# Router logits of an attention and expert kernel: split fp32r products against fp32 products in four column quarters

## The chip, the cores and the metric

The kernel runs on one core of one Trainium2 chip. The time is the device time of one execution in microseconds (us), the median of several executions.

## The reference

Eight batches of eight heads of causal attention over 576 positions of 64 numbers, then a two-level mixture of experts on the 4,608 resulting tokens of 512 numbers. All is fp32.

```python
s_pos = np.maximum(s, 0.0); cum = np.cumsum(s_pos, axis=-1)
bias = -(cum[:, :, :, None] - cum[:, :, None, :])
scores = np.where(causal, -1e9, scale * q @ k.T + np.minimum(bias, 0.0))
attn = softmax(scores)                       # max taken off, 1e-9 in the sum
x = (attn @ v) as tokens                     # [4608, 512]
g_logits = x @ w_group                       # 4 groups: argmax and softmax weight
e_logits = x[of group g] @ w_expert[g]       # 4 experts of the group: the same
h = np.maximum(x[of expert] @ w1[g, e], 0.0) # 512 -> 1024
out[of expert] = (g_w * e_w)[:, None] * (h @ w2[g, e])
```

So each token needs 20 logits (4 of the groups, 4 x 4 of the experts), goes through one of 16 experts, and its row is scaled by the product of two softmax weights.

## The kernel before

**Number forms.** TensorE takes fp32 operands whole, or in the form fp32r, which holds fewer bits. Where the kernel wants the accuracy of fp32 from fp32r it splits an operand into a high part (the cast to fp32r) and a low part (the rest) and adds the products high x high, high x low and low x high.

**Attention.** Two heads make a pair; there are 32 pairs, four to a batch. A loop over steps (`for step in [-4, -3] + list(range(NH + 5))`) interleaves several heads: the row maxima of the head four steps on (line 208), the scores of this head (lines 265 and 267), the exponentials (line 275) and the causal zeroes on GpSimd (line 284), and the product with V of the head before (line 305). The order is written out by hand: `ORDERS` holds a list for even and one for odd steps, in which a token with a digit issues one group of matmuls (A row maxima, B scores, C product with V) and a letter pops one deferred piece of work from a queue of its own. `R` takes one turn of the router. PE, DVE, ACT and Pool follow the order in which they are issued; each engine is a queue in order. `ring` hands out the three score banks in turn and first pops the reader of the bank three before. ScalarE's queue also issues two small DMAs a pair (line 243).

**Tokens.** When a pair is done, `turn`, `recip`, `back` and `finish` (letters Y, Z, W, K) make its tokens transposed, `xT`, 128 channels x 576 positions, on VectorE (line 352). Then `high` casts 512 positions to fp32r on ScalarE (X, line 365), `low` subtracts on GpSimd (L, line 370; VectorE for the last two pairs), `tail` copies the last 64 positions on ScalarE (M, line 375), and `rows_out` turns the pair back to rows on TensorE and stores them (O and o, lines 393 and 399). After the fourth pair of a batch, `route` (Q) queues a router batch.

**The router.** `Router.batch` is a generator; each `R` runs it to the next `yield`. `logits` (lines 720, 721, 724) adds eight fp32r matmuls of 512 columns: for each of the four 128-channel chunks the high tokens against high and low weights side by side (52 columns, the low ones from column 32) and the low tokens against the high weights (20 columns). ScalarE copies rows 32 to 52 out (`lo`, line 780), VectorE adds them to rows 0 to 20 (line 782). The 64 tail positions are four fp32 products (line 785) and a copy (line 786). Then the tails are turned to rows and stored (lines 791 to 798), the logits `lT` are turned to tokens in rows by five transposes against the identity (line 803), and VectorE picks groups and experts, counts, and makes lists of tokens (lines 811 to 947). For the last batch the logits of three chunks are issued one pair early.

**Between the stages.** The first expert slot starts while the last batch is routed. Its matmuls and the router's are put in one order of TensorE with `behind(later, earlier)`: the 41st, 53rd and 73rd product of its first layer stand behind the last logits, their turn and the counts, and the ninth of its second layer behind the first list.

**The slots.** One expert after the other, the fullest first. `x_items` turns the gathered rows on VectorE (line 1111) and splits them (high on ScalarE, line 1115; low on VectorE, line 1116), two channel chunks at a time. `h_items` makes eight 128-row blocks of the hidden layer from `xh` and `xl` and the weights `w.h` and `w.l` (line 1155): four chunks of (xh wh, xl wh), then four of xh wl. ReLU and its split follow (`hh` line 1150, `hl` line 1151). `y_items` makes the output (line 1210), or `y_rows` (line 1177) where the slot's size is a multiple of 128. The next slot's gather, turn and weight split run beside this. `beyond`, five VectorE items (lines 1457 to 1461) that test whether a slot overflows, is issued after the sixth block of slot 3.

Of the kernel before, what the change touches and what calls it, by code (L numbers as in the profile page):

```python
# [20 lines left out]
P = 128  # L21
# [90 lines left out]
def attention(tc, qk, v, s, wr, xs, st):  # L112
# [3 lines left out]
    with ExitStack() as ctx:  # L116
# [207 lines left out]
        def normalise(p, vals, sums):  # L324
# [22 lines left out]
            def finish():  # L347
                for k in "OXLM":
                    need(k, p - 2)
                x = m["x"] = sm.tile([P, S], F32, name=f"xT{p}", tag="xT", bufs=2)  # L350
                xTs[p] = x
                product[0] = nc.vector.tensor_tensor(out=x, in0=vals, in1=m["f"], op=ALU.mult)
                push("X", p, high)
                push("O", p, lambda: rows_out(p))

            def high():
                x = m["x"]
                if c == 0:
                    for k in "LMQ":
                        need(k, p - 1)  # L360
                    rt[0].read(p // 4)
                    xhl[p // 4] = [late.tile([P, 4, 512], F32R, name=f"xT{n}{p}", tag=f"xT{n}", bufs=1) for n in "hl"]
                    xtail[p // 4] = late.tile([P, 4, 64], F32, name=f"xtl{p // 4}", tag="xtail", bufs=2)
                xh, xl = (t[:, c] for t in xhl[p // 4])
                st.xh = nc.scalar.copy(xh, x[:, 0:512])
                st.highs.append(st.xh)
                push("L", p, lambda: low(xh, xl, x))

            def low(xh, xl, x):
                st.lows.append((nc.gpsimd if p < NP - 2 else nc.vector).tensor_tensor(  # L370
                    out=xl, in0=x[:, 0:512], in1=xh.bitcast(F32), op=ALU.subtract))
                push("M", p, lambda: tail(x))

            def tail(x):
                nc.scalar.copy(xtail[p // 4][:, c], x[:, 512:576])
                b = p // 4
                if p == NP - 2:
                    push("Q", p, lambda: rt[0].logits(b, *xhl[b], range(3)))
                if c == 3:
                    push("Q", p, lambda: route(b))  # L380

            push("Y", p, turn)

        def route(b):
            rt[0].queue.append(rt[0].batch(b, xtail.pop(b), *xhl.pop(b)))

        def rows_out(p):

            b, c = p // 4, p % 4
            x = xTs.pop(p)  # L390
# [13 lines left out]
        xTs, xtail, xr, xhl = {}, {}, [None], {}  # L404
# [43 lines left out]
        c0, c1 = (late.tile([P, 4, 512], F32R, name=f"c{n}", tag=f"xT{n}", bufs=1).rearrange("p a c -> p (a c)")  # L448
# [7 lines left out]
        wr_f = ac.tile([P, 4, 20], F32, name="wr_f")  # L456
        wr_sb = ac.tile([P, 4, 52], F32R, name="wr_sb")
        nc.scalar.dma_start(wr_f, wr.rearrange("(c p) n -> p c n", p=P))
# [37 lines left out]
        def constants():  # L496
            ones(3)
            rt.append(Router(tc, ac, late, end, kept, ring, wr_f, wr_sb, xs, st))


        def store_sums():
# [137 lines left out]
class Router:  # L639


    def __init__(self, tc, ac, sm, end, ps_t, ps_s, wr_f, wr_sb, xs, st):
        self.end = end
        self.tc, self.sm, self.ps_t, self.ps_s, self.xs, self.st = tc, sm, ps_t, ps_s, xs, st
        self.wr_f, self.wr_sb = wr_f, wr_sb
# [3 lines left out]
        self.lg = {}  # L649
# [21 lines left out]
        self.lT = ac.tile([20, NB * P], F32, name="lT")  # L671
        nc.gpsimd.memset(self.lT[:, S:], 0.0)
        nc.gpsimd.memset(self.wr_sb.bitcast(F32).rearrange("p c n -> p (c n)"), 0.0)
# [38 lines left out]
    def logits(self, b, xh, xl, chunks):  # L712

        nc = self.tc.nc
        if chunks[0] == 0:
            self.lg[b] = self.ps_s(f"lg{b}")
# [967 lines left out]
```

## Time and profile before

| | us |
|---|---|
| median of 3 runs | 917.94 |
| lowest and highest of them | 917.87, 923.0 |
| the profiled execution | 919.4 |
| its span, first to last instruction | 917.6 |

| engine | busy us | share of the span |
|---|---|---|
| PE (TensorE matmul) | 863.2 | 94% |
| PEld (TensorE weight load) | 777.8 | 85% |
| DVE (VectorE) | 701.0 | 76% |
| ACT (ScalarE) | 628.9 | 69% |
| POOL (GpSimd) | 660.5 | 72% |

Matmuls are pipelined and their ends are modelled, so a PE that is busy all the time is not a PE at its peak: where matmuls follow each other, the distance from start to start is the cost of one, not its length. Time that a DMA issue takes on a queue is not counted as busy. The granted TensorE clock was 0.99 of full speed over the span.

### The profile page before, as it was taken

How to read it: one execution, taken by the hardware profiler on the slowest of the kernel's cores; microseconds unless marked ns; L12 is line 12 of the kernel's file. 1: busy time of each engine (PE TensorE's matmuls, PEld its weight loads, DVE VectorE, ACT ScalarE, POOL GpSimd, SP SyncE). 2: the span in 40 equal slices, each digit the busy share in tenths (PEclk: the TensorE clock that was granted, in tenths of full speed). 3: DMA queues.
4: the chain of work that ended last, by engine and by line, in shares of the span. 5: the costliest groups of instructions: out<-in, count | busy, mean ns of one | idle time of the engine just before them, and what ended most of it. 6: DMA issues, size and time to landing. Idle time of an engine off the chain costs nothing. (4 is left out here: it accounts for less than half of the span.)

```text
span 917.6 us, 17751 instructions
## 1 busy us (share of the span) xinstructions
PE 863.2 (94%) x5649; PEld 777.8 (85%) x5649; DVE 701.0 (76%) x1997; ACT 628.9 (69%) x1374; POOL 660.5 (72%) x762
## 2 busy tenths in 40 slices
PE   4899999999999999999999999999999999999993
PEld 3688787887878788887888999999999999999992
DVE  7776685867868686885676798889888889888830
ACT  3688786887878788876846556665767666676640
POOL 8898686867868687763787565666678878877750
PEclk9999999999999999999999999999999999999997
DMA  7766655563555656423556544554645555665410
GB/s 154 180 168 158 151 142 146 142 163 92 157 151 145 145 144 168 109 85 132 161 215 218 179 163 166 193 187 174 224 175 195 186 208 187 230 229 198 171 44 23
DMA packets 65005, 148.10 MB, mean 161 GB/s; under 512 B 7588, under 2 KB 40996, under 8 KB 54728
## 3 DMA queue, kind: packets, MB, share of 16 engines
q1 hardware_dynamic: 55020, 126.98, 46.3%
q0 software_dynamic: 7488, 18.89, 5.6%
q10 hardware_dynamic: 2396, 1.02, 0.4%
q8 instruction: 47, 0.77, 0.4%
q14 instruction: 54, 0.44, 0.2%
HBM read 108.97 MB, written 19.69 MB: 140 GB/s over the span
## 5 line engine op out<-in xcount | busy, mean ns | idle before, releaser
L1042 POOL TENSOR_TENSOR wl<-raw,wh 128x512 fp32r<-128x512 f32 x182 | 232.1, 1297 | 53.6 <-ACT wh L1039 35.4
L159 POOL TENSOR_TENSOR WB<-r,WA 64x576 fp32r<-64x576 f32 x128 | 180.9, 1413 | 23.4 <-PE pm L208 7.2
L216 DVE CUSTOM_DVE_ANT_0 mx<-pm,mask 128x192 bf16<-128x192 f32 (+4 forms) x320 | 129.1, 419 | 39.2 <-PE pm L208 34.6
L1039 ACT CAST wh<-raw 128x512 fp32r<-128x512 f32 x256 | 153.9, 616 | 1.4 <-issue 0.8
L1155 PE MATMUL ph<-xl,wh 128*128 128x256 f32 (+13 forms) x512 | 145.7, 304 | 5.0 <-DVE xl L1116 4.5
L1155 PE MATMUL ph<-xh,wh 128*128 128x256 f32 (+13 forms) x512 | 144.7, 301 | 1.6 <-ACT xh L1115 1.1
L208 PE MATMUL pm<-WA 66*128 66x288 f32 (+4 forms) x384 | 126.0, 356 | 17.5 <-DMA WA<-ch 9.4
L265 PE MATMUL ps<-WA 68*128 68x320 f32 (+4 forms) x384 | 135.3, 356 | 7.1 <-ACT pu L275 3.7
L305 PE MATMUL po<-pt,VT 128*128 128x256 f32 (+3 forms) x512 | 121.2, 353 | 0.5 <-POOL xTl L370 0.5
L1210 PE MATMUL py<-hl,wh 128*128 128x256 f32 (+13 forms) x448 | 113.3, 302 | 1.3 <-DVE hl L1151 1.3
L1210 PE MATMUL py<-hh,wh 128*128 128x256 f32 (+13 forms) x448 | 112.7, 301 | 0.0
L267 PE MATMUL ps<-WB 128*128 128x320 f32 (+4 forms) x384 | 109.8, 299 | 0.0
L1256 DVE STREAM_TRANSPOSE yr<-yT 32x384 f32<-32x384 f32 (+1 forms) x208 | 104.5, 502 | 4.3
L305 PE MATMUL po<-pu,VT 128*128 128x320 f32 (+1 forms) x384 | 107.3, 388 | 0.0
L1111 DVE STREAM_TRANSPOSE xt<-xg 32x256 f32<-32x256 f32 (+1 forms) x208 | 102.5, 493 | 3.2
L1155 PEld LDWEIGHTS ph<-xl,wh 128*128 128x128 f32 x512 | 96.6, 189 | 8.6 <-DVE xl L1116 6.4
L1155 PEld LDWEIGHTS ph<-xh,wh 128*128 128x128 f32 x512 | 96.7, 189 | 3.8 <-ACT xh L1115 2.7
L305 PEld LDWEIGHTS po<-pt,VT 128*128 128x128 f32 x512 | 87.6, 192 | 12.9 <-issue 0.8
L1150 ACT ACTIVATE hh<-ph 128x256 fp32r<-128x256 f32 (+13 forms) x128 | 53.5, 420 | 61.1 <-PE ph L1155 60.4
L208 PEld LDWEIGHTS pm<-WA 66*128 66x128 f32 (+1 forms) x384 | 68.7, 190 | 30.9 <-DVE mc L216 13.7
L1155 PE MATMUL ph<-xh,wl 128*128 128x256 f32 (+13 forms) x512 | 90.1, 299 | 0.0
L284 POOL TENSOR_SCALAR_AFFINE_SELECT pt<-pt 128x128 f32<-128x128 f32 (+2 forms) x192 | 63.7, 342 | 36.5 <-ACT pt L275 31.9
(256 smaller groups left out, 1913.5 us busy)
## 6 DMA issues: line engine op xcount, KB each, us to landing
raw<-in_w_dram SPq DMA_DIRECT2D x64, 1024.0 KB
WB<-WA SPq DMA_DIRECT2D x64, 288.0 KB
r<-in_qk_dram SPq DMA_DIRECT2D x31, 576.0 KB
VT<-in_v_dram SPq DMA_DIRECT2D x32, 384.0 KB
xs<-xr SPq DMA_DIRECT2D x15, 512.0 KB
xs<-xrt SPq DMA_DIRECT2D x7, 128.0 KB
xg<-xs,ids POOLq DMA_INDIRECT x46
out_dram<-yr,ids POOLq DMA_INDIRECT x43
```

The costliest lines, as they stand in the source:

```text
L159: i = nc.gpsimd.tensor_tensor(out=wb[64 * a:64 * a + 64, a, h], in0=r[:, h, a], in1=w[0:64, a, h, QO:].bitcast(F32), op=ALU.subtract)
L208: nc.tensor.matmul(ps[:rows, :cw], WA[i][0:66, QA, h, QO + q0:QO + q0 + rows], WA[i][0:66, KA, h, QO + c0:QO + c0 + cw], start=True, stop= ...
L216: nc.vector.tensor_tensor_reduce(out=tmp[:rows, :cw], in0=ps[:rows, :cw], in1=mk[:rows], scale=1.0, scalar=-3.0e38 if c0 == 0 else mo, op0 ...
L265: nc.tensor.matmul(ps[:rows, o:o + w], WA[i][0:68, KA, h, QO + k0:QO + k0 + rows], WA[i][0:68, QA, h, QO + q0:QO + q0 + w], start=True, st ...
L267: nc.tensor.matmul(ps[:rows, o:o + w], WB[p % NBB][:, KA, h, k0:k0 + rows], WB[p % NBB][:, QA, h, q0:q0 + w], start=False, stop=True)
L305: i = nc.tensor.matmul(po[0][:, qa - base:qb - base], VT[p % NVT].rearrange("p t a d -> p (t a d)")[:, (3 * t + 1 + h) * 64:][:, 0:P], x[: ...
L1039: self.casts.append(nc.scalar.copy(h[:, j], raw[:, j]))
L1042: self.low = nc.gpsimd.tensor_tensor(out=l[:, j], in0=raw[:, j], in1=h[:, j].bitcast(F32), op=ALU.subtract)
L1111: V.transpose(dst[:, 0:n, :, j], src[:, 0:n, :, i])
L1155: self.products.append(nc.tensor.matmul(pss[f][:, :cap], w[f // 4][:, c, (f % 4) * P:(f % 4 + 1) * P], x[:, c, :cap], start=(c == 0 and w ...
L1210: self.products.append(nc.tensor.matmul(pss[c][:, :cap], w[2 + f // 4][:, f % 4, c * P:(c + 1) * P], x[:, f, :cap], start=(f == 0 and w is ...
L1256: V.transpose(dst[:, 0:n, :, i], src[:, 0:n, :, j])
```

## The change

The tokens are no longer split. One tile `xT` of four pairs holds a batch, and `finish` writes a pair's tokens into it; `high`, `low`, `tail` and `route` are gone, and Q now queues the batch and stands in the even steps, after B0 and ahead of a turn of the router. The logits are fp32 products of chunk c with 32 columns of weights (12 of them zero), written to the partitions 32c to 32c + 32 of a bank; no chunk is added to another on TensorE. Two copies on ScalarE bring the four parts to `lT`, now 128 rows. The turn, five fp32 products against `sum4` in place of the transposes, turns the logits and adds the four parts in one. In `item(0)` of a slot's first layer, and in the first block of `y_rows`, the products with the low tokens (low hidden rows) now come last. `beyond` comes after the second block of slot 3. The counts with which the first slot's matmuls stand behind the router's are 35, 46 and 64, and 4.

```diff
             def finish():
-                for k in "OXLM":
-                    need(k, p - 2)
-                x = m["x"] = sm.tile([P, S], F32, name=f"xT{p}", tag="xT", bufs=2)
-                xTs[p] = x
+                b = p // 4
+                if c == 0:
+                    rt[0].read(b - 1)
+                    need("O", p - 5)
+                    xTs[b] = late.tile([P, 4, S], F32, name=f"xT{b}", tag="xT", bufs=2)
+                x = xTs[b][:, c]
                 product[0] = nc.vector.tensor_tensor(out=x, in0=vals, in1=m["f"], op=ALU.mult)
-                push("X", p, high)
                 push("O", p, lambda: rows_out(p))
-            def high():
...
-                st.xh = nc.scalar.copy(xh, x[:, 0:512])
...
-                st.lows.append((nc.gpsimd if p < NP - 2 else nc.vector).tensor_tensor(
-                    out=xl, in0=x[:, 0:512], in1=xh.bitcast(F32), op=ALU.subtract))
...
-                nc.scalar.copy(xtail[p // 4][:, c], x[:, 512:576])
...
                 if c == 3:
-                    push("Q", p, lambda: route(b))
+                    push("Q", p, lambda: rt[0].queue.append(rt[0].batch(b, xTs[b])))
...
-            "b S R B0 R v b a A0 B2 v C0 e G a R a B3 T C1 A3 B1 A2 C2 b e t R C3 v G C4 B4 J b D v e a R a A1 "
+            "b S R B0 Q R v b a A0 B2 v C0 e G a R a B3 T C1 A3 B1 A2 C2 b e t R C3 v G C4 B4 J b D v e a R a A1 "
...
+        nc.gpsimd.memset(wr_f[:, :, 20:32], 0.0)
...
-            V.tensor_copy(self.wr_sb[:, :, 0:20], self.wr_f)
-            V.tensor_tensor(out=self.wr_sb[:, :, 32:52], in0=self.wr_f, in1=self.wr_sb[:, :, 0:20].bitcast(F32),
-                            op=ALU.subtract)
+            V.tensor_reduce(out=self.sum4, in_=self.st.ident.rearrange("p (c n) -> p n c", c=4)[:, 0:20], axis=AX.X, op=ALU.add)
...
+    def logits(self, b, x):
+        nc, lT = self.tc.nc, self.lT
+        out = []
+        for a, e in ((0, 512), (512, S)):
+            ps = self.ps_s(f"lg{b}_{a}")
+            for c in range(4):
+                i = nc.tensor.matmul(ps[32 * c:32 * c + 32, 0:e - a], self.wr_f[:, c], x[:, c, a:e], start=True, stop=True)
+            out.append((lT[:, a:e], ps[:, 0:e - a]))
+        for o, ps in out:
+            nc.scalar.copy(o, ps)
+        self.st.logged = i
...
-        lg = self.logits(b, xh, xl, range(3, 4) if b in self.lg else range(4))
-        lo = sm.tile([20, 512], F32, name=f"lo{b}", tag="lo", bufs=1)
-        nc.scalar.copy(lo, lg[32:52])
-        yield
-        V.tensor_tensor(out=lT[:, 0:512], in0=lg[:20], in1=lo, op=ALU.add)
-        ps = self.ps_s(f"pl{b}")
-        for c in range(4):
-            nc.tensor.matmul(ps[:20, :64], self.wr_f[:, c], xtail[:, c], start=(c == 0), stop=(c == 3))
-        nc.scalar.copy(lT[:, 512:S], ps[:20, :64])
+        self.logits(b, x)
         yield
...
-            st.turned = nc.tensor.transpose(ps[:, t * 20:(t + 1) * 20], lT[:, t * P:(t + 1) * P], ident[:20, :20])
+            st.turned = nc.tensor.matmul(ps[:, t * 20:(t + 1) * 20], lT[:, t * P:(t + 1) * P], self.sum4,
+                                         start=(t == 0), stop=(t == NB - 1))
...
                 def item(f):
+                    if f == 0:
+                        pss[f] = acc(f"ph{u}_{f}")
+                        for c0 in (0, 2):
+                            for w in (self.w.h, self.w.l):
+                                for c in (c0, c0 + 1):
+                                    product(f, w, self.xh, c, False)
+                        for c in range(4):
+                            product(f, self.w.h, self.xl, c, c == 3)
+                        relu(f)
+                        return
                     first(f)
                     last(f)
...
+                    if t == 0:
+                        terms = [(f, n) for f, n in terms if n < 2] + [(f, 2) for f in range(8) if f0]
...
-        run(wts[0].load((st.evacs[-3], st.xh, st.xrt, st.xrt), (first.last,) * 4, nc.gpsimd))
+        run(wts[0].load((st.evacs[-3], st.evacs[-1], st.xrt, st.xrt), (first.last,) * 4, nc.gpsimd))
...
-            behind(tc, made[40], st.logged)
-            behind(tc, made[52], st.turned)
-            behind(tc, made[72], st.counted)
+            behind(tc, made[34], st.logged)
+            behind(tc, made[45], st.turned)
+            behind(tc, made[63], st.counted)
...
-            behind(tc, made[8], st.listed[0])
+            behind(tc, made[3], st.listed[0])
...
-                    if i == 5 and k == 3:
+                    if i == 1 and k == 3:
                         beyond()
```

## Rows read from the trace of the kernel before

**Rows 1.** Busy time by stretch: us, then PE, PEld, DVE, ACT, POOL, clock, DMA.
```profile
93.20:411.20 318.00, 308.04 (x1935) 257.24 (x1933) 239.57 (x933) 254.09 (x582) 235.58 (x328) 0.99 0.53 137
470.00:917.60 447.60, 423.92 (x2920) 410.15 (x2918) 354.44 (x691) 273.59 (x568) 307.94 (x256) 0.99 0.50 178
```

**Rows 2.** PE groups by shape, whole span: count, busy us, mean ns of one, idle before.
```profile
L305 PE MATMUL po<-pu,VT 128*128 128x320 f32 x256 | 82.3, 443 | 0.0
...
L305 PE MATMUL po<-pu,VT 128*128 128x128 f32 x128 | 25.0, 277 | 0.0
```

**Rows 3.** PE in order of time, a head with logits.
```profile
306.70 0.41 PE L720 MATMUL lg<-xTh,wr_sb 128*52 128x512 f32 x1
...
308.57 0.29 PE L208 MATMUL pm<-WA 66*128 66x288 f32 x1
...
309.88 0.62 PE L785 MATMUL pl<-xtl,wr_f 128*20 128x64 f32 x8
310.43 0.39 PE L265 MATMUL ps<-WA 68*128 68x256 f32 x1
...
313.67 0.42 PE L265 MATMUL ps<-WA 68*128 68x320 f32 x1 [0.35 <-ACT pu L275]
...
314.82 0.49 PE L803 MATMUL plt<-ident,lT 20*128 20x20 f32 x5
315.24 0.76 PE L305 MATMUL po<-pt,VT 128*128 128x192 f32 x4
```

**Rows 4.** Busy time by stretch: a pair without logits, a head with them.
```profile
294.90:306.50 11.60, 11.60 (x77) 10.17 (x75) 8.05 (x32) 10.14 (x24) 9.43 (x14) 1.00 0.55 134
306.50:316.40 9.90, 9.28 (x63) 6.75 (x61) 3.75 (x17) 6.96 (x17) 6.63 (x11) 1.00 0.63 158
```

**Rows 5.** ACT in order of time, a pair without logits: start us, us, operation, [idle].
```profile
293.26 0.62 ACT L365 CAST xTh<-xT 128x512 fp32r<-128x512 f32 x1
293.79 0.58 ACT L399 COPY xr<-px 128x512 f32<-128x512 f32 x1
294.26 0.44 ACT L275 ACTIVATE pu<-ps 128x320 f32<-128x320 f32 x1
...
295.33 0.24 ACT L375 COPY xtl<-xT 128x64 f32<-128x64 f32 x1
295.59 0.38 ACT L314 ACTIVATE sums<-po 64x256 f32<-64x256 f32 x1
...
299.84 0.72 ACTq L243 DMA_DIRECT2D WA<-th  x1
...
300.66 0.89 ACTq L243 DMA_DIRECT2D WA<-tl  x1
```

**Rows 6.** Waits, 480 to 917.6 us: us in total, times, longest.
```profile
PEld ph L1155 <- DVE xl L1116: 6.4, 9, 1.2
...
PE py L1210 <- DVE hl L1151: 1.3, 2, 1.0
```

**Rows 7.** All engines in order of time, the head of slot 4.
```profile
585.46 1.57 DVE L1116 TENSOR_TENSOR xl<-xt,xh 128x644 fp32r<-128x644 f32 x2
...
585.49 0.41 PE L1155 MATMUL ph<-xh,wh 128*128 128x322 f32 x1
...
586.35 0.42 PE L1155 MATMUL ph<-xl,wh 128*128 128x322 f32 x1 [0.45 <-DVE xl L1116]
```

**Rows 8.** Groups by shape, all engines, 144.6 to 399.4 us; columns as rows 2.
```profile
L370 POOL TENSOR_TENSOR xTl<-xT,xTh 128x512 fp32r<-128x512 f32 x20 | 25.5, 1275 | 24.3 <-ACT xTh L365 24.3
...
L782 DVE TENSOR_TENSOR lT<-lg,lo 20x512 f32<-20x512 f32 x5 | 3.4, 679 | 0.0
...
L780 ACT COPY lo<-lg 20x512 f32<-20x512 f32 x5 | 2.9, 577 | 5.2 <-PE lg L724 5.2
...
L786 ACT COPY lT<-pl 20x64 f32<-20x64 f32 x5 | 1.0, 202 | 0.0
```

**Rows 9.** PE in order of time, first slot: the last batch's first list.
```profile
463.78 0.56 PE L899 MATMUL pi<-val,rows 128*128 128x128 bf16 x5 [1.60 <-DVE val L892]
```

More of the change, by code (lines that the diff above doesn't have):

```diff
@@ L347, in finish @@
             def finish():
-                for k in "OXLM":
-                    need(k, p - 2)
-                x = m["x"] = sm.tile([P, S], F32, name=f"xT{p}", tag="xT", bufs=2)
-                xTs[p] = x
+                b = p // 4
[4 more added lines that the diff above has]
+                x = xTs[b][:, c]
                 product[0] = nc.vector.tensor_tensor(out=x, in0=vals, in1=m["f"], op=ALU.mult)
-                push("X", p, high)
                 push("O", p, lambda: rows_out(p))
-            def high():
[L357 to L364, printed above, removed]
-                st.xh = nc.scalar.copy(xh, x[:, 0:512])
-                st.highs.append(st.xh)
-                push("L", p, lambda: low(xh, xl, x))
-            def low(xh, xl, x):
-                st.lows.append((nc.gpsimd if p < NP - 2 else nc.vector).tensor_tensor(
-                    out=xl, in0=x[:, 0:512], in1=xh.bitcast(F32), op=ALU.subtract))
-                push("M", p, lambda: tail(x))
-            def tail(x):
-                nc.scalar.copy(xtail[p // 4][:, c], x[:, 512:576])
-                b = p // 4
-                if p == NP - 2:
-                    push("Q", p, lambda: rt[0].logits(b, *xhl[b], range(3)))
                 if c == 3:
-                    push("Q", p, lambda: route(b))
+                    push("Q", p, lambda: rt[0].queue.append(rt[0].batch(b, xTs[b])))
             push("Y", p, turn)
-        def route(b):
-            rt[0].queue.append(rt[0].batch(b, xtail.pop(b), *xhl.pop(b)))
         def rows_out(p):
             b, c = p // 4, p % 4
-            x = xTs.pop(p)
+            x = xTs[b][:, c]
             ps = ring(f"px{p}", "o", True)
@@ L447, in attention @@
         BH = B * H
-        c0, c1 = (late.tile([P, 4, 512], F32R, name=f"c{n}", tag=f"xT{n}", bufs=1).rearrange("p a c -> p (a c)")
+        c0, c1 = (late.tile([P, 4, S], F32R, name=f"c{n}", tag="xT", bufs=2).rearrange("p a c -> p (a c)")
                   for n in "hl")
@@ L455, in attention @@
         load_raw(1)
-        wr_f = ac.tile([P, 4, 20], F32, name="wr_f")
-        wr_sb = ac.tile([P, 4, 52], F32R, name="wr_sb")
-        nc.scalar.dma_start(wr_f, wr.rearrange("(c p) n -> p c n", p=P))
+        wr_f = ac.tile([P, 4, 32], F32, name="wr_f")
+        nc.scalar.dma_start(wr_f[:, :, 0:20], wr.rearrange("(c p) n -> p c n", p=P))
         def ones(i):
@@ L497, in constants @@
             ones(3)
-            rt.append(Router(tc, ac, late, end, kept, ring, wr_f, wr_sb, xs, st))
+            rt.append(Router(tc, ac, late, end, kept, ring, wr_f, xs, st))
         def store_sums():
@@ L710, in read @@
             self.step(True)
[L712 to L716, printed above, removed]
-        ps = self.lg[b]
-        for c in chunks:
-            if c < 3:
-                nc.tensor.matmul(ps[:52], self.wr_sb[:, c], xh[:, c], start=(c == 0), stop=False)
-            nc.tensor.matmul(ps[:20], self.wr_sb[:, c, 0:20], xl[:, c], start=False, stop=False)
-        if chunks[-1] == 3:
-            self.logged = b
-            self.st.logged = nc.tensor.matmul(ps[:52], self.wr_sb[:, 3], xh[:, 3], start=False, stop=True)
-            return self.lg.pop(b)
+    def logits(self, b, x):
[9 more added lines that the diff above has]
+        self.st.logged = i
     def pick(self, k, bank):
@@ L761, in second, with batch @@
         V.tensor_tensor(out=st.count, in0=st.count, in1=t, op=ALU.add)
-    def batch(self, b, xtail, xh, xl):
+    def batch(self, b, x):
         tc, sm, st = self.tc, self.sm, self.st
```

32 lines of the change are left out of this document (17 added, 15 removed), and 2 rows, old and new, of the table ORDERS.

## The prediction

> **What bounds the kernel now.** I read the stretches first. Attention from 93 to 411 us and the expert slots from 470 us on are 765 of the 917.6 us, and TensorE is busy for 97% and 95% of them [rows 1]. But matmuls overlap, so busy is not full, and I worked out the price of a column. An fp32 matmul goes from 277 to 443 ns between 128 and 320 columns, 0.865 ns a column [rows 2]. Eight fp32r ones of 512 columns take 1.87 us, 0.457 ns a column [rows 3]. An fp32 product is two such matmul instructions: the four tail products of a batch (line 785) stand as x8 in [rows 3]. A head has 1,600 columns of row maxima, 3,200 of scores (both fp32r, 2.19 us) and 1,600 of probabilities times V in fp32 (3,200 instruction columns, 2.77 us). A pair of heads with its four transposes and one of the maxima (128 columns, 0.11 us each) is 2 x 4.96 + 0.55 = 10.5 us.
>
> A quiet pair takes 11.60 us [rows 4]. So TensorE has some 1.1 us to spare there, and something else sets the pace. It is ScalarE: busy 10.14 us of the 11.60, and its two DMA issues of 0.72 and 0.89 us stand in the same queue [rows 4, 5]; one operation of 0.44 us ran beside them. The reader is to see in [rows 5] that each ScalarE instruction starts where the one before ends, first of all the high copy and the tail copy of the tokens. The head that carries the logits takes 9.90 us [rows 4], half of a quiet pair being 5.80; there ScalarE is busy only 6.96 and TensorE is the late one: its logits, tails and turn are 1.87 + 0.55 + 0.42 = 2.84 us in [rows 3].
>
> In the expert stage TensorE waits at the head of a slot for the low half of the tokens: weight loads 6.4 us, nine times [rows 6]. In [rows 7] the first product starts at 585.49 and the second, on the low half, at 586.35.
>
> **The change, part by part.** *ScalarE, each pair.* The high copy leaves: 293.26 to 293.79, 0.53 us from start to start. So does the tail copy: 295.33 to 295.59, 0.26 us [rows 5]. Together 0.79 us of a queue that is full. What is late next is TensorE at 10.5 us, so there is room for all of it. But chains through banks and row maxima also hold it, and in the one head of eight that carries logits ScalarE is not late. Bounds: nothing, and 28 x 0.79 = 22 us (32 pairs less the four of the start-up). I take 70%: **-15.5 us**. The removed work cannot cost.
>
> *GpSimd and VectorE.* GpSimd loses 1.28 us a pair, VectorE 0.68 us a batch (the sum of high and low) [rows 8]. Neither sets the pace of a quiet pair: GpSimd waited for the high copy before each low one, 24.3 us in all [rows 8]. I cost both at nothing; ScalarE and TensorE cover them.
>
> *ScalarE, each batch.* The low-logit copy (0.58) and tail copy (0.20) go [rows 8]; a 128x512 and a 128x64 copy come, by the nearest rows 0.58 and 0.24 [rows 5, 8]. Zero in work. They stand ahead of the next head's evacuations, and the score bank after next needs an exp behind them. Today's wait of that kind is 0.35 us [rows 3]. Bounds: nothing, and the two copies, an evacuation of sums (0.38) and an exp (0.44) [rows 5] on an idle TensorE, 1.6 us. I take 0.5, nearer today's row: **+4 us** for eight batches.
>
> *TensorE, each batch.* Eight fp32r matmuls (1.87) and the 20-row tails (0.55) become eight fp32 instructions of 512 columns (0.443 us each by the slope) and eight of 64 (0.055), in four column quarters. No row shows two quarters at once. Above: one after another, 3.54 + 0.44 us. Below: all four beside each other, only the two instructions of one chunk in turn, 0.89 + 0.11. The rows have nothing between these ends, but the code does: the two instructions of a chunk share a quarter, and the next chunk's first comes behind them. If TensorE keeps its order, only the second of one chunk can run beside the first of the next: five turns of eight, 2.21 + 0.28 = 2.49 us. I take that, the middle. The turn becomes five fp32 products of 128 rows, ten loads and matmuls at 0.084 (0.42/5 in [rows 3]), 0.84 us. Sum 3.33 against 2.84: **+3.9 us** for eight batches; ends -8.0 and +15.8. The Trainium skill (TensorE: Matmul & The Clock Gate, Part 3: Packing small matmuls) says outputs at 32-partition offsets run concurrently and that three column tiles gained 2.38x, while matmuls start and end in strict order, and no row of this trace shows the first of the two. By its 2.38x, an estimate, the quarters would take 3.98/2.38 = 1.67 us and the whole 6.6 us less than mine, between my case and the side-by-side rival below.
>
> *Queues.* No DMA is added. The store of the last 64 rows of a batch goes out on SP one router turn sooner; its queue is not late. Logits move from the end of an odd step to after the first scores of the next even step, behind the cast of the raw keys and queries on ScalarE, while TensorE streams them. The tokens' tile of a batch is written over that of two batches before, whose readers ended a whole batch earlier. The setup makes one sum over the identity in place of two operations on the router's weights: nothing, in the start-up.
>
> *Slots.* High products with high and low weights now come first, the low tokens at the ninth. A product of 322 columns streams for 0.147 us, so they are wanted at 585.49 + 8 x 0.147 = 586.67 [rows 7]; VectorE has both halves at 585.46 + 1.57 = 587.03, the first near 586.25. A rest of some 0.15 us stays for the second half. 6.4 us less nine rests: **-5 us** (bounds 0 and -6.4). The weights' low halves are wanted sooner; [rows 6] has no wait of TensorE for them. The overflow test moves four items forward in slot 3: it stands on VectorE before the last low hidden rows, and the wait for those is 1.3 us [rows 6]; **-1 us**.
>
> *Between the stages.* TensorE stands 1.60 us at the last batch's lists [rows 9]; that chain loses a split and a sum, though all its logits now follow its last tokens. **-1 us** (0 and -1.6; if the logits serialise it is later by about as much).
>
> *Sum.* -15.5 + 4 + 3.9 - 5 - 1 - 1 = -14.6 us. The profiled execution took 919.4 us (span 917.6): 904.8. It is 1.5 us above the median of 917.94, so 903.3 there: **903 us**.
>
> **Rivals.** *Quarters in turn* (24%): TensorE takes the eight instructions one by one. The row that speaks for it: the eight narrow tails of [rows 3], start to start 0.07 us, one after the other, though on the same columns. +11.9 us on mine and about 2 more for later copies: 917 us.
>
> *All four at once* (12%): the chunks' first instructions run together, then the second ones. -11.9 us: 891 us.
>
> *ScalarE's time is not paid out* (12%): TensorE and VectorE wait for each other through the two banks of row maxima, and a quiet pair stays near 11.6 us. For it: TensorE's busy 11.60 of 11.60 in [rows 4]. Against: ScalarE's unbroken chain [rows 5]. The 15.5 us stay away: 918.5 us.
>
> *Slower* (10%): the logits step takes the place of what ScalarE gave. The block of serial quarters (+1.98 us with the turn) holds up the scores, and the next scores then wait for both copies, an evacuation and an exp (1.6 us): 3.6 us a batch, 29 us. ScalarE's gain then counts only in three pairs of four, 11.6 us. 919.4 + 29 - 11.6 - 7 - 1.5 = 928 us. It decides from 2.8 us a batch on, where eight batches use up the 22.5 us of gains. In its favour: the logits head already costs 4.1 us more than a quiet one [rows 4] for 2.84 us of logits work. The Trainium skill (TensorEngine Tiling (Array Packing), Key Properties) says a change of tiling mode drains the engine. A drain by rows is about 277 - 111 = 0.17 us [rows 2], twice a batch 2.7 us in all: it helps this rival and does not decide it.
>
> **How the numbers follow.** My own case has 42%, from 895 to 911 us. Under 1% is what a measurement here cannot tell from no change: 908.8 to 927.1 us. Faster: nine tenths of my case, all of the side-by-side case, and some 6% from the two near 918: 0.56. Slower: most of the last rival and edges of the others: 0.09. Same: 0.35. The range goes from 892, in the side-by-side case, to 922, above the two near 918; some 2 in 10 lie outside, most of it in the slower rival and the low end.
>
> **What would show it.** A quiet pair at 10.8 to 11.1 us with ScalarE still unbroken shows the first step; 11.6 refutes it. The eight 512-column quarter matmuls from first start to the next work: 2.2 us is mine, 3.5 the serial rival, 0.9 the best case. A logits head above 10.5 us with TensorE idle for an exp behind the two copies shows the slower rival. In the slots the wait for the low tokens falls from 6.4 to about 1.5 us; if a wait for low weights or high tokens takes its place, that term is wrong. My forecast is wrong most simply if ScalarE's 0.79 us turns into idle ScalarE.

## The result, and the profile after

The changed kernel took 928.31 us, the median of four runs (925.72 to 931.89), against 917.9 us for the kernel before beside it: a ratio of 1.0105, 95% interval 1.006 to 1.015. It is 10 us slower, where 903 was predicted, and outside the range of 892 to 922. The profiled execution took 931.89 us, its span is 930.1; it is the slowest of the four, 3.6 us above the median, so its sums explain 12.5 us and not 10.

I read the stretches first: the row of [rows 1] for attention, then the end of attention, the start of the first slot up to its first output product, and the slots. The columns are from and to, us, then busy time of PE, PEld, DVE, ACT and POOL, granted clock, DMA share, GB/s. Before, where [rows 1] does not have them:

```profile
411.20:443.00 31.80, 30.27 (x192) 24.16 (x190) 18.16 (x55) 23.05 (x63) 13.48 (x28) 1.00 0.39 130
443.00:461.10 18.10, 17.52 (x144) 15.44 (x143) 14.20 (x57) 14.00 (x34) 16.57 (x15) 1.00 0.63 206
461.10:917.60 456.50, 431.22 (x2980) 417.08 (x2978) 361.70 (x720) 274.54 (x571) 314.86 (x262) 0.99 0.50 178
```

After, the same four stretches:

```profile
93.20:415.50 322.30, 309.38 (x1959) 260.36 (x1957) 233.84 (x922) 239.34 (x531) 201.04 (x302) 0.97 0.52 135
415.50:446.20 30.70, 29.07 (x196) 23.67 (x195) 16.46 (x53) 20.79 (x53) 9.80 (x23) 1.00 0.38 132
446.20:475.70 29.50, 20.45 (x155) 18.35 (x153) 21.60 (x84) 10.70 (x29) 13.74 (x12) 0.82 0.41 139
475.70:930.10 454.40, 434.19 (x2973) 420.51 (x2973) 352.80 (x690) 276.31 (x575) 317.36 (x264) 0.98 0.50 178
```

Attention up to its last head is 4.3 us longer, though ScalarE is busy 15 us less in it; its end wins 1.1. The start of the first slot takes 29.5 us in place of 18.1, 11.4 more: that alone is more than the loss. The slots win 2.1. Together 12.5 us, the difference of the two spans. (Both rows of attention start at 93.2 us; what was won or lost ahead of that is in the first of them.)

**The first slot.** PE, then ACT, in order of time, after:

```profile
475.67 0.58 PE L1191 MATMUL py<-hh,wh 128*128 128x256 f32 x1 [6.31 <-ACT wh L1002]
```

```profile
467.56 1.82 ACT L1116 ACTIVATE hh<-ph 128x256 fp32r<-128x256 f32 x4 [6.21 <-PE ph L1121]
474.90 0.17 ACT L899 CAST pk<-c 128x15 f32<-128x15 bf16 x1 [5.51 <-DVE c L898]
475.00 6.33 ACT L1002 CAST wh<-raw 128x512 fp32r<-128x512 f32 x12
```

TensorE stands 6.31 us for the first expert's second-layer weights (w2). Their casts stand in ScalarE's queue behind the router's last cast (line 899), which waits for VectorE; ScalarE idles 6.21 and 5.51 us ahead of them. Before, the eight casts ran ahead of the last hidden activations:

```profile
454.35 2.18 ACT L1039 CAST wh<-raw 128x512 fp32r<-128x512 f32 x4 [0.54 <-ACT pk L890]
...
456.63 2.16 ACT L1039 CAST wh<-raw 128x512 fp32r<-128x512 f32 x4
459.82 1.82 ACT L1150 ACTIVATE hh<-ph 128x256 fp32r<-128x256 f32 x4 [1.02 <-PE ph L1155]
```

The change edits neither these eight casts nor the gate (`st.xrt`) that they wait behind. The rest of the 11.4 us is a wait of TensorE of 1.8 us for GpSimd (`val`), one of 0.5 us for VectorE, and the clock: from 458.2 to 465.0 us the granted clock was 0.50, that is 1.2 GHz. It was 0.50 again from 471.8 us, within the stand, to 482.0.

**The logits head.** PE in order of time, after; it answers to [rows 3]:

```profile
254.90 1.18 PE L690 MATMUL lg<-xT,wr_f 128*32 128x512 f32 x16
256.01 0.40 PE L208 MATMUL pm<-WA 66*128 66x288 f32 x1
256.67 0.47 PE L265 MATMUL ps<-WA 68*128 68x448 f32 x1 [0.26 <-ACT lT L693]
...
260.96 1.27 PE L765 MATMUL plt<-sum,lT 128*128 128x20 f32 x10
262.07 0.22 PE L208 MATMUL pm<-WA 66*64 66x64 f32 x1
263.15 0.47 PE L208 MATMUL pm<-WA 66*128 66x448 f32 x1 [0.85 <-DVE mc L216]
```

VectorE at the same place:

```profile
262.26 0.26 DVE L774 TENSOR_REDUCE lmx<-plt 128x25 f32<-128x100 f32 x1 [2.08 <-PE plt L765]
```

All sixteen instructions of a batch's logits, tails included, take 1.11 us (254.90 to 256.01): the quarters run beside each other. The turn takes 1.11 us too. VectorE stands 2.08 us for it, with the next row maxima queued behind, and then TensorE stands 0.85 us for a row maximum. Now the stretches of a quiet pair ahead of the first logits (before, then after), and after of the pair of [rows 4] and of the head behind the logits:

```profile
75.90:87.40 11.50, 11.16 (x72) 9.77 (x71) 7.96 (x31) 10.14 (x23) 10.78 (x15) 1.00 0.54 143
75.80:86.70 10.90, 10.90 (x72) 9.73 (x71) 7.86 (x31) 9.59 (x21) 9.61 (x14) 1.00 0.61 152
295.40:307.20 11.80, 11.76 (x76) 10.14 (x76) 8.39 (x34) 9.61 (x21) 8.24 (x12) 1.00 0.49 131
262.10:270.50 8.40, 7.54 (x38) 6.19 (x37) 6.37 (x24) 4.64 (x11) 3.62 (x5) 0.80 0.49 118
```

The pair of [rows 4] went from 11.60 to 11.80 although ScalarE lost work there. In the head behind the logits the granted clock averages 0.80: part of it ran at 1.2 GHz in place of 2.4, after TensorE had run the ten narrow products of the turn and stood still. That head takes 8.4 us, in batches that keep the clock 6.75. In this execution that happened behind five of the six logits heads inside attention, in that of before behind two. Three more at 1.6 us are 4.9 us, more than the 4.3 us by which attention is longer. Where the clock stayed full, a batch of eight heads takes 52.6 us after (163.8 to 216.4) and 52.4 before (217.8 to 270.3), though ScalarE is busy 40.2 us in it in place of 42.7.

**The slots.** Waits from 480 us to the end (us, times, longest); the last row answers to [rows 6]:

```profile
PEld py L1191 <- DVE hl L1117: 4.2, 9, 1.2
PEld ph L1121 <- ACT xh L1078: 3.6, 7, 0.8
PEld ph L1121 <- DVE xl L1079: 1.2, 4, 0.4
```

The wait for low tokens fell from 6.4 to 1.2 us as forecast, and waits for high tokens and for low hidden rows (2.7 and 2.0 us before) took part of its place.

### The profile page after: what moved, and what is told of

Same layout as the page of the kernel before. It is cut to its first block, busy times and chain, and to the rows that moved or that the text cites. A ratio compares the mean times of both kernels' runs of the same rounds, so it can differ in the third digit from the quotient of the medians.

```text
span 930.1 us, 17673 instructions
## 1 busy us (share of the span) xinstructions
PE 870.8 (94%) x5689; PEld 788.6 (85%) x5689; DVE 690.0 (74%) x1986; ACT 609.7 (66%) x1310; POOL 620.1 (67%) x732
## 5 line engine op out<-in xcount | busy, mean ns | idle before, releaser
L208 PE MATMUL pm<-WA 66*128 66x288 f32 (+4 forms) x384 | 129.6, 363 | 22.0 <-DVE mc L216 10.5
L1121 PE MATMUL ph<-xh,wh 128*128 128x256 f32 (+13 forms) x512 | 142.7, 305 | 2.6 <-ACT xh L1078 1.9
L1121 PE MATMUL ph<-xl,wh 128*128 128x256 f32 (+13 forms) x512 | 139.7, 304 | 0.3
L1191 PE MATMUL py<-hh,wh 128*128 128x256 f32 (+13 forms) x448 | 116.0, 307 | 6.3 <-ACT wh L1002 6.3
L1191 PE MATMUL py<-hl,wh 128*128 128x256 f32 (+13 forms) x448 | 117.1, 308 | 2.3 <-DVE hl L1117 2.0
L208 PEld LDWEIGHTS pm<-WA 66*128 66x128 f32 (+1 forms) x384 | 70.8, 194 | 35.9 <-DVE mc L216 18.6
L275 ACT ACTIVATE pt<-ps 128x256 f32<-128x256 f32 (+2 forms) x192 | 76.5, 399 | 25.7 <-PE ps L267 12.1
```

What stands on the lines that cost most here:

```text
L208: nc.tensor.matmul(ps[:rows, :cw], WA[i][0:66, QA, h, QO + q0:QO + q0 + rows], WA[i][0:66, KA, h, QO + c0:QO + c0 + cw], start=True, stop= ...
L1121: self.products.append(nc.tensor.matmul(pss[f][:, :cap], w[f // 4][:, c, (f % 4) * P:(f % 4 + 1) * P], x[:, c, :cap], start=(c == 0 and w ...
L1191: self.products.append(nc.tensor.matmul(pss[c][:, :cap], w[2 + f // 4][:, f % 4, c * P:(c + 1) * P], x[:, f, :cap], start=(f == 0 and w is ...
```

## The experiments

Runs made together share a chip and its runs of before; across groups of runs I compare ratios to before. The groups are e1 to e4, e5 to e8, e9 to e12 and e13 to e15.

**Two pools that overlap.** The change took `xT` (2 x 2,304 bytes) out of the pool `sm`. The pools lie one behind the other, so `late`, which holds the router's tiles, moved down by 4,608 bytes: it starts at 173,760 bytes of a partition in place of 178,368. The expert stage's pool `x2`, which holds the raw w2, ends at 175,360 and now overlaps it by 1,600 bytes.

The idea to be tested is that the planner, which orders ScalarE here, puts the w2 casts behind the router's last cast because of this overlap. That it does so because it frees a pool as a whole, and not for a tile that both still use, is my reading; no run shows it.

e1_gap:

```diff
         sm = ctx.enter_context(tc.tile_pool(name="sm", bufs=2))
+        sm.tile([P, 448], F32, name="gap", tag="gap", bufs=1)
         late = ctx.enter_context(tc.tile_pool(name="late", bufs=1))
```

> The changed kernel with one unused tile of 1,792 bytes at the end of the pool sm, so that the pool late starts at 175,552 bytes, above the end of the pool x2 (175,360), as it did before the change (178,368); in the changed kernel it starts at 173,760, below that end. Nothing that is computed differs. Theory (the two pools overlap by 1,600 bytes, so the first expert's w2 casts are ordered behind the router's last read of its tiles): the 6.31 us stand of TensorE before the first slot's second product is gone, the eight w2 casts come before the last hidden activations, and the time falls by 8 to 11 us from 928.3, to 917 to 920. Rival (the column quarters, the longer turn and the halved clock in attention are the loss): at most 2 us come back, 926 or more.

Measured: 922.13 us, ratio 1.0044 (1.0025 to 1.0062), 0.61 points or 5.6 us better than the change. PE's waits from 443 to 482 us, and ScalarE:

```profile
PE pw L863 <- POOL val L908: 3.1, 1, 3.1
```

```profile
453.51 4.26 ACT L1003 CAST wh<-raw 128x512 fp32r<-128x512 f32 x8 [0.60 <-ACT xrt L755]
...
466.21 1.82 ACT L1117 ACTIVATE hh<-ph 128x256 fp32r<-128x256 f32 x4 [5.35 <-PE ph L1122]
```

The 6.31 us stand is gone and the casts are early again. A bit less came back than expected, because the next wait shows: 3.1 us for GpSimd, which e5 takes up.

e2_late_before:

```diff
-                x = m["x"] = sm.tile([P, S], F32, name=f"xT{p}", tag="xT", bufs=2)
+                x = m["x"] = late.tile([P, S], F32, name=f"xT{p}", tag="xT", bufs=2)
```

> The kernel before with one word changed: the pair's token tile xT is taken from the pool late instead of sm, so that late starts at 173,760 bytes as in the changed kernel and overlaps x2. Same instructions. Theory of the overlapping pools: slower by 8 to 11 us, 926 to 929, with TensorE standing some 6 us for a w2 cast at the first slot's second product. Rival: 918, no change.

Measured: 926.93 us, ratio 1.009 (1.0063 to 1.0116). One word in the kernel before makes it nearly as slow, with the same kind of wait:

```profile
PE py L1210 <- ACT wh L1039: 5.9, 1, 5.9
```

So the cause of this wait is shown from both sides: where the pools lie, not the instructions.

**The slots alone.** e3_slots_only puts the diff's hunks of `h_items`, `y_rows` and `beyond` into the kernel before.

> The kernel before with the slots' part of the change alone (low tokens last in the first hidden item, low hidden rows last in the first output rows, the overflow test at item 1 of slot 3). Theory (the slots gain what the two traces show from the first output product on): 2 to 5 us faster, 913 to 916, the wait of weight loads for the low tokens from 6.4 to about 1.5 us. Rival (the new order wants the weights' low halves or high tokens too early and gives nothing): 917 to 919.

Measured: 916.82 us against 918.65, ratio 0.9976 (0.9959 to 0.9992): 1.8 us by the medians, 2.2 by the ratio, the least that was expected. Waits of weight loads: low tokens 1.2 us, but high tokens 4.1 and low hidden rows 4.2.

**VectorE's load.** e4_gap_pool:

```diff
-                    if b < B - 1 and j == 0:
+                    if b < B - 1:
```

> e1_gap, and the two products of the gate weights that VectorE makes in each of the first seven batches go to GpSimd too. Theory (in the heads that carry router work VectorE's queue sets the pace, which eats what ScalarE gave back): 0.96 us less VectorE a batch, 4 to 7 us faster than e1_gap. Rival (those heads are late by the halved clock and by TensorE's own waits, not by VectorE's load): within 1.5 us of e1_gap.

Measured: 921.58 us, ratio 1.003 (1.0013 to 1.0046), 0.5 us from e1_gap by the medians, within its interval. The theory fell in this form: the head that lost 0.58 us of VectorE's work stayed at 6.4 us, and the next one became 0.2 us shorter. Between the stages the wait for `val` grew to 4.5 us. Not VectorE's load as such, but what stands in front of what in its queue, was the next idea.

**The gate.** e5_gate, on e1_gap; `st.left` is the last copy in `leave`:

```diff
-        run(wts[0].load((st.evacs[-3], st.evacs[-1], st.xrt, st.xrt), ...
+        run(wts[0].load((st.evacs[-3], st.left, st.xrt, st.xrt), ...
```

> e1_gap, and the casts of the first expert's second piece (wh_1) are ordered behind the last copy of the tokens to their store (which stands where the high copy stood that gated them before the change) instead of behind the last evacuation of row sums. By that GpSimd makes the gate-weight product of batch 6 before the low parts of that piece, as before the change, and not behind them. Theory: TensorE's 3.13 us wait for that product and the stretch of half clock behind it (0.50 from 456 to 460 us) go; 4 to 6 us faster than e1_gap (922.1), 916 to 918. Rival (GpSimd's order is not what TensorE waits for): 921 to 923.

Measured: 918.5 us, ratio 1.001 (0.9987 to 1.0033): 0.34 points, 3.1 us better than e1_gap; the two intervals overlap. TensorE no longer waits for GpSimd's product; 0.9 and 0.8 us for VectorE are late next. The first slot is not mended by that: from its first product to its first output product it takes 22.4 us (24.2 in e1_gap, 18.1 before), at a granted clock of 0.85. The change had named another gate for the casts of the second piece of w1 because the old one, the high copy, no longer exists, and by that put a product that TensorE wants behind eight low parts of GpSimd. In the changed kernel's trace:

```profile
445.36 10.59 POOL L1005 TENSOR_TENSOR wl<-raw,wh 128x512 fp32r<-128x512 f32 x8 [4.45 <-ACT wh L1002]
455.91 0.71 POOL L907 TENSOR_TENSOR val<-col,c 128x320 bf16<-128x320 bf16 x1
```

**The turn.** e6_turn_early, on e5_gate:

```diff
         st.xrt = (nc.scalar if b == B - 1 else nc.sync).dma_start(...)
-        yield 1
+        yield
 ...
                                          start=(t == 0), stop=(t == NB - 1))
+        yield
         G = [P, NB * 5, 4]
```

> e5_gate, with the turn of the logits issued one router step earlier and its readers on VectorE where they were. Theory: in the logits head VectorE stands 2.1 us for the turn with the next row maxima queued behind it, TensorE then stands 0.86 us for a row maximum, and the granted clock falls to 0.5 right behind; with the turn done earlier VectorE's wait falls below 0.7 us, TensorE's goes, and fewer of the seven batches show the half clock (a batch of 54.1 us becomes 52.4 or less): 7 to 13 us faster than e5_gate. Rival (the half clock comes from the turn's ten small matmuls themselves, wherever they stand): within 2 us of e5_gate, as many batches at 54.

Measured: 908.99 us against e5's 918.5 beside it, ratio 0.9908 (0.9881 to 0.9934). 9.5 us faster, by two lines. VectorE and TensorE:

```profile
254.73 0.26 DVE L776 TENSOR_REDUCE lmx<-plt 128x25 f32<-128x100 f32 x1 [1.41 <-PE plt L766]
```

```profile
253.50 1.19 PE L766 MATMUL plt<-sum,lT 128*128 128x20 f32 x10
...
255.62 0.47 PE L209 MATMUL pm<-WA 66*128 66x448 f32 x1 [0.19 <-DVE mc L217]
```

VectorE's wait fell only to 1.4 us, but that was enough for TensorE, whose 0.85 us became 0.19. The granted clock over three batches after, and then over two in e6:

```profile
109.80:163.80 54.00, 51.80 (x330) 43.75 (x329) 39.06 (x155) 40.57 (x90) 34.79 (x52) 0.97 0.55 141
163.80:216.40 52.60, 50.44 (x331) 42.44 (x329) 38.99 (x156) 40.19 (x90) 34.34 (x51) 1.00 0.57 144
216.40:270.50 54.10, 51.93 (x331) 43.56 (x329) 39.06 (x155) 40.29 (x90) 34.63 (x51) 0.97 0.54 141
```

```profile
105.98:157.78 51.80, 50.28 (x330) 42.52 (x329) 38.95 (x155) 40.31 (x90) 34.66 (x51) 1.00 0.56 147
157.78:209.55 51.77, 50.26 (x331) 42.51 (x329) 38.95 (x155) 40.35 (x90) 34.65 (x51) 1.00 0.58 146
```

A batch lost 0.8 us where the clock had been full and 2.2 to 2.4 where it had not: with the stand the half clock went too.

e7_turn_read_late has only the second of the two hunks.

> e5_gate, with the turn where it is and its readers on VectorE one router step later, behind the row maxima (all later router steps move by one). Theory: as e6_turn_early, VectorE does not stand for the turn: 5 to 13 us faster than e5_gate. Rival (small matmuls lower the clock): within 2 us of e5_gate, as many batches at 54.

Measured: 909.33 us, ratio 0.9912 (0.9889 to 0.9935). The turn stands where it stood and is as long; only its reader comes later, and the gain is the same; TensorE does not stand behind the turn, and the half clock shows behind none of the six heads. So the narrow products by themselves do not lower the clock here; the stand behind them belongs to it.

**The quarters.** e8_one_quarter, on e5_gate:

```diff
-                i = nc.tensor.matmul(ps[32 * c:32 * c + 32, 0:e - a], ..., start=True, stop=True)
+                i = nc.tensor.matmul(ps[0:32, 0:e - a], ..., start=(c == 0), stop=(c == 3))
```

> e5_gate, with the four chunks of a batch's logits accumulated in one quarter of 32 columns, one after the other, in place of four; the rest stands (the copies are of 32 rows). Theory (it is the separate quarters that let the products run beside each other): the 16 instructions take 3.5 to 4.0 us in place of 1.11, the logits head is up by 2 to 2.9 us, the kernel by 12 to 23 us. Rival (fp32 products of few columns overlap anyway): 1.1 us, no change.

Measured: 932.24 us, ratio 1.0162 (1.0129 to 1.0195), 13.7 us slower than e5_gate. The sixteen instructions, 204.17 to 208.16, take 3.99 us:

```profile
204.17 4.07 PE L691 MATMUL lg<-xT,wr_f 128*32 128x512 f32 x16
208.16 0.40 PE L209 MATMUL pm<-WA 66*128 66x288 f32 x1
```

That is the price one after the other that the prediction had worked out (3.54 + 0.44 us). The same work in four quarters takes 1.11 us, 3.6 times less. The stand of TensorE behind the turn is still 0.86 us in this kernel, yet the half clock shows behind only one of its six logits heads. So that stand does not always bring it; what else decides was not tried.

**The same turn on the old logits.** e9_before_turn makes the edit of e6_turn_early in the kernel before.

> The kernel before with the turn of the logits issued one router step earlier (the edit of e6_turn_early, on the old logits). VectorE waits 1.76 us for the turn there too, but TensorE stands only 0.28 and 0.37 us for row maxima behind it, and only two of seven batches of the profiled run had the half clock. Theory (the stand is what the change made worse, and ScalarE paces the other heads of before): 2 to 5 us faster than before, 912 to 915, so that e6's gain is for the smaller part one that the old logits could have too. Rival (the early turn is worth as much there): 8 us or more, 909 or less.

Measured: 909.83 us against 919.52, ratio 0.9907 (0.9883 to 0.993). The rival is right: the early turn is worth as much without the change. The logits head falls from 9.85 to 8.82 us, the next from 6.3 to 6.09, and the half clock shows behind none:

```profile
247.50:256.32 8.82, 8.82 (x63) 6.66 (x61) 3.78 (x18) 6.65 (x16) 5.62 (x10) 1.00 0.68 171
256.32:262.41 6.09, 5.89 (x38) 5.13 (x37) 5.80 (x23) 5.03 (x12) 4.31 (x5) 1.00 0.36 78
```

TensorE's stands of 0.28 and 0.37 us behind the turn are gone. A batch falls from 52.4 us at full clock to 51.2 (205.1 to 256.3), so here most of the gain is not the clock, which only two batches of before had lost.

e10_no_slots is e6_turn_early without the slots' part.

> e6_turn_early without the slots' part of the change. Theory (that part is worth what e3_slots_only measured on the kernel before, 2 us, since the stages meet only at one point): 910.5 to 912. Rival (the parts depend on each other): outside 909 to 914.

Measured: 911.22 us, ratio 0.9915 (0.9894 to 0.9937), beside e9's 909.83; against e6 it is 2.2 us slower by the medians, 0.6 by the ratios. With the early turn on both sides the new logits by themselves give nothing; they are level with the old ones or 1 us behind. Part of that is still the first slot: from its first product to its first output product it takes 22.7 us here and 18.1 in e9.

**ScalarE's time by itself.** e11_scalar_back, on e6_turn_early; `spare` is a tile of its own:

```diff
+                push("X", p, lambda: nc.scalar.copy(spare[:, 0:512], x[:, 0:512]))
+                push("M", p, lambda: nc.scalar.copy(spare[:, 512:S], x[:, 512:S]))
```

> e6_turn_early with the two ScalarE copies that the change took out of each pair put back (128x512 and 128x64 of the tokens into a tile that nothing reads), at their old places. This prices ScalarE's time alone. Theory (with the turn out of the way TensorE and VectorE leave less than ScalarE's 0.79 us a pair to win, and most pairs carry router work on VectorE): 3 to 8 us slower than e6_turn_early, 912 to 917. Rival (the prediction's term: 70% of 0.79 us in each of 28 pairs): 13 to 18 us slower, 922 to 927. Second rival (ScalarE's time is worth nothing): within 1.5 us.

Measured: 910.23 us, ratio 0.9903 (0.988 to 0.9925), against e6's 0.9908. The second rival: 0.79 us of ScalarE in each of 32 pairs cannot be told from nothing (1.2 us slower than e6 by the medians, 0.5 faster by the ratios). A quiet pair of the first batches, then two pairs with router work, in e6 and in e11:

```profile
63.34:74.27 10.93, 10.93 (x72) 9.76 (x71) 7.88 (x31) 9.62 (x21) 8.39 (x13) 1.00 0.72 193
209.55:222.22 12.67, 12.03 (x84) 10.31 (x82) 11.05 (x46) 9.80 (x22) 8.38 (x14) 1.00 0.50 116
222.22:234.38 12.16, 11.95 (x77) 10.13 (x76) 10.79 (x43) 10.06 (x24) 9.81 (x14) 1.00 0.68 194
```

```profile
65.01:76.56 11.55, 11.19 (x72) 9.80 (x71) 8.00 (x31) 10.14 (x23) 8.30 (x13) 1.00 0.67 185
212.13:224.80 12.67, 12.02 (x83) 10.30 (x82) 11.06 (x46) 10.36 (x24) 8.38 (x14) 1.00 0.46 109
224.80:236.70 11.90, 11.87 (x77) 10.25 (x76) 10.21 (x43) 10.28 (x25) 9.84 (x14) 1.00 0.69 192
```

The quiet pair pays 0.6 us. The first pair with router work pays nothing and the second is 0.26 us shorter; the third (not shown) is 0.17 us longer. Each batch in the steady state has three such pairs beside the one with logits; quiet are only the pairs ahead of the first logits. A batch stays at 51.7 us.

**Late next.** e12_weights_direct, on e6_turn_early:

```diff
-                                                    in1=c3p[:, j]...
+                                                    in1=(c3 if b == B - 2 else c3p)[:, j]...
```

> e6_turn_early, and in batch 6 VectorE reads the split gate weights from SBUF in place of the copy that ScalarE puts into PSUM. Between the stages VectorE stands 2.14 us for that copy, and TensorE then 0.79 and 0.92 us for VectorE, with the clock at 0.59 from 446 to 450 us. Theory (that wait is on the path): 1.5 to 4 us faster than e6_turn_early, 905 to 907.5. Rival (something else ends last there): within 1 us, 908 to 910.

Measured: 906.62 us, ratio 0.9871 (0.985 to 0.9892), 2.4 us better than e6 by the medians, 3.4 by the ratios. That wait was on the path: the first slot's stretch falls from 20.9 us in e6 to 17.9, as before the change, at full clock.

e13_copies_on_vector, on e12:

```diff
-            nc.scalar.copy(o, ps)
+            nc.vector.tensor_copy(o, ps)
```

> e12_weights_direct, with the two copies of the logits out of PSUM on VectorE in place of ScalarE. In the logits head TensorE stands 0.26 us for a score bank behind these copies, and VectorE is busy only 3.1 of its 8.97 us. Theory (the copies in ScalarE's queue are what keeps the shorter logits from shortening that head): the head falls from 8.97 to 8.6 or less, the kernel by 2 to 3 us, to 904 to 905. Rival (VectorE stands for the logits with its row maxima behind, as it did for the turn): the head stays at 8.9 or longer, 906 or more.

Measured: 904.04 us, ratio 0.9856 (0.9839 to 0.9873). The logits head, e12 and then e13:

```profile
246.53:255.50 8.97, 8.53 (x67) 6.67 (x66) 2.85 (x13) 6.14 (x15) 4.55 (x8) 1.00 0.62 168
```

```profile
245.38:253.83 8.45, 8.28 (x67) 6.63 (x66) 3.57 (x15) 5.44 (x13) 4.55 (x8) 1.00 0.69 176
```

0.52 us a batch: ScalarE's copies ahead of the scores did hold up TensorE. The kernel gained 2.6 us on e12 by the medians and 1.4 by the ratios, on another chip. e14_logits_at_old_place, on e12, moves the letter `Q` back to the end of the odd step.

> e12_weights_direct, with the logits queued at the end of the odd step again, as before the change, so that they and all router steps behind them come one place earlier. Theory (the place among the scores, not the logits' length, sets the logits head): 8.97 falls to about 8.2 us, what e9's 8.82 gives less 1.3 us of shorter logits and tails plus 0.6 us of a longer turn; 4 to 6 us faster, 901 to 903. Rival (the tokens' product of VectorE, which the logits read, comes just before that place and TensorE then stands for it): a wait of TensorE for xT, 907 to 912.

Measured: 906.56 us, ratio 0.989 (0.9873 to 0.9907). The logits head fell as the theory has it, to 7.98 us, and no wait for the tokens came; the gain still stayed away, because the router's later steps now stand beside other work: the next head rose from 6.09 to 6.85 us, two others from 6.42 and 5.75 to 7.2 and 6.8, two fell, and the batch stayed at 51.8.

e15_old_logits_best is e9 with the slots' part and the edit of e12.

> e9_before_turn with the slots' part of the change and the direct read of the gate weights in batch 6: everything found here on the old split logits. Theory (the new logits give nothing of their own: e10 911.2 against e9 909.8): 905 to 908, level with e12_weights_direct or up to 2 us faster. Rival (the new logits are worth something once the rest is mended): 909 or more.

Measured: 907.07 us, ratio 0.9895 (0.9878 to 0.9911), 3 us behind e13 on the same chip. So the new logits are worth some 3 us at most, once their copies are off ScalarE's queue; before that it cannot be told from nothing (e14 is 0.5 us ahead of e15 on the same chip, e12 2.2 by ratios whose intervals overlap). The old ones' copies were left there. The traces say where the gain lies: e13's batches are as long as e15's (51.2 us at their shortest), but its first logits head starts at 91.6 us against 93.3. Most of that is won in the quiet pairs ahead of it, where ScalarE's time is paid out. e13 beats both kernels, by 1.4% the one before.

## Why the prediction was wrong

**ScalarE, -15.5 us.** This is the step that failed in the sum: that 70% of the 0.79 us taken off ScalarE is paid out in each of 28 pairs. Its chain in [rows 5] is unbroken, and I took the pattern of 28 pairs from one. Put back by itself, ScalarE's time costs 1 us or nothing (e11). It is paid out ahead of the first logits, where a quiet pair went from 11.5 to 10.9 us and the first logits head starts 2 us earlier (91.2 us in e1_gap, 93.2 before); in the batches behind, which are as long as before at full clock, it is not. The first sentence against it stood in my own rows: TensorE was busy 11.60 of 11.60 us in [rows 4]. I priced that pair's TensorE work at 10.5 us from the attention matmuls alone. It holds a product of the router's lists as well, which stands in TensorE's row of before from 295.07 to 295.69:

```profile
295.07 0.69 PE L899 MATMUL pw<-val,rows 128*128 128x192 bf16 x5
295.69 0.40 PE L208 MATMUL pm<-WA 66*128 66x288 f32 x1
```

And a quiet pair takes 10.9 us after the change with TensorE busy all through, not 10.5. With the 0.62 us of the list that is 11.5 of the 11.60 us, so there was next to nothing to spare. In the steady state no pair is quiet, that of [rows 4] included. By my own sign (10.8 to 11.1 us, or 11.6) the quiet pairs ahead of the first logits bear the step out, and the pair of [rows 4], at 11.8, refutes it. "ScalarE's time is not paid out", the rival with 12%, names the mechanism.

**Copies, +4 us.** Right in kind and size: e13 took 0.52 us off each logits head, 3.1 us over the six inside attention.

**TensorE's logits, 2.49 us a batch.** Wrong, on the good side: 1.11 us, as in the rival of four at once. The rule of the Trainium skill (TensorE: Matmul & The Clock Gate, Part 3: Packing small matmuls) that outputs at 32-partition offsets run concurrently is borne out, and more strongly than its 2.38x for three tiles: 3.6 for four. **The turn, 0.84 us,** was 1.11. Together 1.1 us a batch less than I charged, and none of it shows in the length of a batch. That VectorE's queue and the copies set the pace in that head instead is what e6 and e13 point to. I had costed the turn as TensorE's work and not asked who stands waiting for it; in the trace of before VectorE waits 1.76 us for it as well. That wait, with the clock that goes with it, is worth some 9 us (e6, e9).

**Slots, -5 us.** -2.2 (e3). The wait for low tokens did go, and I did not ask what is late next: the high tokens and low hidden rows.

**Between the stages, -1 us.** This is the other step that failed, and alone as large as the whole loss. The stretch became 11.4 us longer. Nothing in the prediction looked there: I followed the router's chain, and not the orders that the planner makes, which rest on where tiles lie. The overlap is worth 5.6 us mended in the changed kernel and 8 us made in the one before (e1, e2), the gate 3.1 us (e5), a wait of VectorE for ScalarE's copy 2.4 to 3.4 us (e12). My "slower" rival named 928 us and a wait of 3.6 us at the logits of every batch; the time fits by chance, the wait is 0.26 us.

So from the change to e5, some 9 us come back that were lost between the stages. What is left, e5's 1.001, is the slots' gain of some 2 us against a loss of some 3. In the profiled executions the first slot starts 0.8 us later than before (443.8 against 443.0 us), with the half clock behind four of six logits heads in place of two, and reaches its first output product 4.3 us later still; 2.5 us of that come back in the rest of that slot.

**Open.** Why the clock falls behind some logits heads and not behind others with the same stand (e8) is not settled; it does behind five in the trace of the change, and behind four in e1 and e5, whose attention is the same. Nor is what holds the heads with router work at 6.2 to 6.4 us: less VectorE work (e4) took 0.2 us off a batch, and another order of steps (e7, e14) or more ScalarE work (e11) left it between 51.6 and 52.2.

## What to carry to other kernels

Where a planner orders an engine, look up which pools lie over which before and after a change of any tile's size or pool: an overlap of 1,600 bytes can tie a stage's start to the end of the one before. A resource that is busy without a break is worth its time only where the others have room in the same stretch, so price it in every kind of stretch, and by adding work to it in one run. Of a step that another engine reads, ask first what is queued behind the reader.

## What the hardware showed

Sixteen fp32 matmul instructions in four 32-column quarters took 1.11 us, in one quarter 3.99 us. The move from such quarters to whole tiles and back left no gap that the rows show: two such instructions of 512 and two of 64 columns alone are 1.0 us, an estimate from the slope of [rows 2]. A stand of 0.85 us behind ten narrow products was followed by 1.2 GHz in some batches, at a cost of 1.6 us each (8.4 against 6.75 us): behind 16 of 24 logits heads in the traces of the change, e1, e4 and e5, but behind one of six in e8. With stands of 0.28 and 0.37 us behind five products it was three of 18 (before, e2, e3), and with a stand of 0.19 us or none, in e6, e7 and e9 to e15, none of 54.
